# A retention and feed-forward kernel: the first weight tiles and item loads in another order, later loads of q and k, and one subtraction moved in the A stages

## The chip, the cores and the metric

The kernel runs on one core of a Trainium2 chip. The metric is the device time of one execution in microseconds. Three runs of the kernel before took 859.01, 855.62 and 859.25 us, median 859.01 us. TensorE (PE, and PEld for its weight loads) multiplies; VectorE (DVE), ScalarE (ACT) and GpSimd (POOL) work on tiles; SyncE (SP) issues nearly all DMAs, ACT a few.

## The reference

```python
scores = np.matmul(q, k.transpose(0, 1, 3, 2)) / np.sqrt(D)      # q, k, v: 8 batches, 8 heads, 576 positions, 64
gamma = 1.0 - 2.0 ** (-5.0 - np.arange(H))
Dmat = np.where(rel >= 0, gamma[:, None, None] ** rel, 0.0)      # rel = position of q - position of k
x = np.matmul(scores * Dmat, v)                                  # then 4608 tokens x 512
h = x @ w_in                                                     # w_in: 512 x 2048
out = (h - np.tanh(h)) @ w_out                                   # w_out: 2048 x 512
```

All inputs and the output are float32.

## The kernel before

The 576 positions are cut into nine chunks of 64. An *item* is one batch in one chunk; eight items make a block of 512 tokens. Retention is computed chunk by chunk: scores inside the chunk, masked by the decay, times v, plus q times a state that the chunks before have left. Float32 products on TensorE are made of two words each: a high word (`xh`, `gh`, the first of `win`) and a low word (the rest, by a subtraction on DVE), three products a term.

**The start.** `load_first` (line 560) loads item j of chunk 0 into `a`; the masks' table `decay` and item 1 go through ACT's queue, everything else through SP's. TensorE first runs matmuls on a zero tile `warm` (`busy`, line 551). Then for each j the loop at line 596 runs the scores of item j + 2 together with the product of item j (`run`, line 300), multiplies scores by the decay (`after_score`, DVE, line 308) and copies the product to `xh` on ACT and its remainder to `xl` on DVE (`after_out`, lines 326 to 329). Meanwhile `load_w` (line 96) loads the tiles of `w_in`, each 128 x 512 of 8 bytes. A tile is made into words in steps: `guard` (two activations on ACT, lines 106 and 111), three bit operations on DVE (lines 137, 145 and 147, in `unit`), a rounded copy on ACT (line 153), and the subtraction for the low word on DVE (line 166, `finish`). `step` does the next piece of that work wherever it is called, so its place in the program is its place in each engine's order. Tile 1 has a function of its own, `second` (lines 124 to 129). Then `mm1` (line 447) multiplies a block by a tile of `w_in`, 12 matmuls of 128 x 512; the program for chunks 0 and 1 runs 32 of these with steps of the tiles to come between them. `behind` makes a DMA wait for a named instruction, and `pace` holds the names.

**The later stages.** Chunks 3 to 8 are handled in pairs: a stage A (`stage_a`) computes the hidden layer of two chunks together from seven products (`product`, line 917) of half blocks, and a stage B (`stage_b`) computes the output of the second chunk while it prepares the next two by attention steps (`attend`). In stage A, pair j leaves two of its four hidden tiles (`c12`, `c22`) in memory and splits the other two into words at once; the fourth of pair 0 (`c21`) is split in a function `rest` that waits in `pending` for pair 1. `u2` and `u4` are sums kept in the tile `work`. In stage B, each step f runs the 12 matmuls of `mm2` (line 503); an even step begins with an attention step. `load_turn` (line 801) loads q and k (in an even step) or v (odd) for an attention step three turns ahead, and is held by a matmul of the step's `mm2`; `fetch` (line 472) loads a hidden tile `s` for four steps ahead, behind it on SP's queue. `scale_q` (line 255) and `split` (lines 932, 933) are the first users of these.

In all of this each engine executes its instructions in the order of the program.

Of the kernel before, what the change touches and what calls it, by code (L numbers as in the profile page):

```python
# [9 lines left out]
F32 = mybir.dt.float32  # L10
F32R = mybir.dt.float32r
I32 = mybir.dt.int32
BF16 = mybir.dt.bfloat16
AF = mybir.ActivationFunctionType
ALU = mybir.AluOpType
# [59 lines left out]
def retention_ffn(ctx: ExitStack, tc: tile.TileContext, ins, out, spill, wvar):  # L75
# [36 lines left out]

    halves = (slice(0, DM // 2), slice(DM // 2, DM))

    def second(low):

        t, f = stream[1]
        hw, lw, z = wraw[t, f][:, :, 1], wraw[t, f][:, :, 0], masks.pop((t, f))
        del wraw[t, f]

        w = const.tile([P, 2, 2, DM // 2], F32R, tag="wi14", name="wi1")
        win[f] = w
        upto("guard", 3)
        nc.vector.scalar_tensor_tensor(z, hw, 3, z, op0=ALU.logical_shift_left, op1=ALU.bitwise_and)
        low()
        nc.vector.scalar_tensor_tensor(z, lw, 29, z, op0=ALU.logical_shift_right, op1=ALU.bitwise_or)
        nc.vector.scalar_tensor_tensor(z, hw, -0x40000000, z, op0=ALU.bitwise_and, op1=ALU.bitwise_or)
        for n, at in enumerate(halves):
            nc.scalar.copy(w[:, n, 0], z[:, at].bitcast(F32))  # L129
        last.append(("i", w, z))  # L130

    def unit(k):

# [29 lines left out]
    def finish():  # L163
        while last:
            hi, lo, full = words_of(*last.pop())
            nc.vector.tensor_tensor(lo, full, hi.bitcast(F32), op=ALU.subtract)
# [7 lines left out]
    def upto(what, n):  # L174
        while at_[what] < min(n, 2 * NF):
            {"load": load_w, "guard": guard}[what](*stream[at_[what]])
            at_[what] += 1
# [117 lines left out]
    def run(same, other):  # L295

        while same or other:
            for ms in (same, other):
                for out_, w, x, start, stop in ms[:2]:
                    nc.tensor.matmul(out_, w, x, start=start, stop=stop)  # L300
                del ms[:2]
# [249 lines left out]
    def busy(n, cols):  # L551
        for _ in range(n):
            nc.tensor.matmul(wps[:, :cols], warm[:, :P], warm[:, :cols], start=True, stop=True)

    busy(WARM, 140)
    busy(8, BLK // 2)
    decay = const.tile([P, 4, C], F32, tag="wo7", name="decay")
    krows = [const.tile([P, 4, 4, D], F32, tag=f"wo{4 + t}", name=f"krows{t}") for t in range(2)]

    def load_first(j, queue=nc.sync):  # L560
        loaded[j] = const.tile([P, 3, 4, C], F32, tag=f"wo{NF - 1 - j}", name=f"a{j}")
        queue.dma_start(loaded[j], first_d[j])

    load_first(0)
    nc.scalar.dma_start(decay, decay_d)
    load_first(1, nc.scalar)
    load_first(2)
    upto("load", 1)
    load_first(3)
    load_first(4)  # L570
    load_first(5)
    nc.scalar.activation(warm[:, :1], warm[:, :1], AF.Tanh)

    firsts, lows = {}, []

    def score_first(j):
        firsts[j] = psp.tile([P, 8, C], F32, tag=("o0", "o1", "h")[j % 3], bufs=(1, 1, 2)[j % 3], name=f"s_first{j}")
        firsts[j] = firsts[j][:, :4]  # L580
        return m_score(j, firsts[j])

    def paced(load):

        pace.append(tc.nc.cur_bb.bb.instructions[-1].name)
        load()

    def load_paced(j):
        load_first(j)
        behind(tc, pace[-1])  # L590

    run(score_first(0), [])
    after_score(0, firsts[0].unsqueeze(1), 1)
    run(score_first(1), [])
    after_score(1, firsts[1].unsqueeze(1), 1)
    for j in range(B):
        o = psp.tile([P, 8, C], F32, tag=("o2", "o3", "own")[j % 3], bufs=1, name=f"own_first{j}")[:, :4]
        run(score_first(j + 2) if j < B - 2 else [], m_out(j, o))
        if j == 0:
            paced(lambda: load_paced(6))  # L600
        if j == 1:
            paced(lambda: load_paced(7))
        if j < B - 2:
            after_score(j + 2, firsts[j + 2].unsqueeze(1), 1)
            if 0 < j < 5:
                paced(lambda: upto("load", j + 1))
        if j == 4:
            nc.sync.dma_start(vtab, vtab_d)
            nc.sync.dma_start(krows[0], krows_d[0])
            load_pair(B)  # L610
            nc.sync.dma_start(mask, mask_d)
            upto("load", 7)
            load_pair(B + 2)
        if j == 3:
            busy(6, BLK)
        if 0 < j < 4:
            step()
        low = after_out(j, o.unsqueeze(1), 1, False)
        if j == 0:
            upto("guard", 1)  # L620
        if j == 3:
            step()
        if j == 5:
            finish()
            guard(*stream[1], both=False)
        if j < 7:
            low()
        else:
            guard_end(masks[stream[1]])
            at_["guard"] = 2  # L630
    units(1)
    second(low)
    at_["convert"] = 2

    def scale_k(t):
# [319 lines left out]
    def stage_a(na):  # L955

        nb, pending = na + 1, []
        u2, u4 = work[:, 0], work[:, 1]
        for j in range(NPAIR):
            x, y = [psp.tile([P, BLK], F32, tag=t, bufs=1, name=f"p{t}{na}_{j}") for t in ("new" if j else "o0", "own")]  # L960
            z, v = [psp.tile([P, BLK], F32, tag="h", bufs=2, name=f"p{t}{na}_{j}") for t in "zv"]
            f1, f2 = 2 * j, 2 * j + 1
            c22, c12, c21 = [pool.tile([P, BLK], F32, tag="g", bufs=3, name=f"c{t}_{na}_{j}") for t in (22, 12, 21)]

            def tanh(c):
                th = pool.tile([P, BLK], F32, tag="cv", bufs=4, name=f"th{na}_{j}")
                nc.scalar.activation(th, c, AF.Tanh)  # L967
                return th

            def away(c, f):  # L970
                nc.gpsimd.tensor_tensor(c, c, tanh(c), op=ALU.subtract)  # L971
                nc.sync.dma_start(spill[nb, f], c)

            product(0, x)
            product(1, y)
            nc.scalar.copy(u2, x)
            nc.vector.tensor_tensor(u2, y, u2, op=ALU.add)  # L977
            product(2, z)
            nc.vector.tensor_tensor(u4, z, u2, op=ALU.add)
            while pending:  # L980
                pending.pop()()
            product(3, v)
            nc.vector.tensor_tensor(c22, v, u4, op=ALU.add)  # L983
            y = psp.tile([P, BLK], F32, tag="own", bufs=1, name=f"py{na}_{j}")
            product(4, y)
            away(c22, f2)
            nc.vector.tensor_tensor(c12, y, u4, op=ALU.add)
            product(5, x, False)
            away(c12, f1)
            g11 = tanh(x)  # L990
            nc.vector.tensor_tensor(g11, x, g11, op=ALU.subtract)
            product(6, v, False)
            split(na, f1, g11, False)
            nc.vector.tensor_tensor(c21, v, u2, op=ALU.add)

            def rest(f=f2, c=c21, tanh=tanh):
                nc.vector.tensor_tensor(c, c, tanh(c), op=ALU.subtract)
                split(na, f, c, True)

            if j == 0:  # L1000
                pending.append(rest)
            else:
                mm2_pair(na, j - 1)
                rest()
        for f in range(3):
            fetch(nb, f)
        mm2_pair(na, NPAIR - 1)
        for f in range(2):
            split(nb, f, fetched.pop((nb, f)), False)
# [5 lines left out]
    def stage_b(n, m0):  # L1015

        fetch(n, 3)
        for f in range(NF):
            def ahead():
                if f + 2 < NF:  # L1020
                    split(n, f + 2, fetched.pop((n, f + 2)), f % 3 == 0)

            if n == 2 and f == 1:
                load_tables(FIRST)
            m, odd = m0 + f // 2, f % 2 == 1
            if n < NC - 1 and not odd:
                attend(m, ahead)
            else:
                ahead()
            if n == NC - 1:  # L1030
                fetch_on(n, f + 4)
            if n == 2 and f == NF - 1:
                load_slot(2)
            if (n, f) != (NC - 1, NF - 2):
                names = mm2(n, f)
            if n < NC - 1:
                load_turn(m + 3 - odd, int(odd), names[6 if odd else 2])
                fetch_on(n, f + 4)
            if odd and tables:
                load_tables(tables.pop())  # L1040
                set_tables()
            if n == 2 and f == 2:
                set_tables()
            if n == 2 and 9 < f < 15:
                load_slot(*((0, f - 10) if f < 14 else (1,)))
# [87 lines left out]
```

## Time and profile before

| | |
|---|---|
| median of three runs | 859.01 us (855.62 to 859.25) |
| the profiled execution's own time | 856.53 us |
| its span | 854.8 us |
| TensorE busy | 843.2 us (99%), 7701 matmuls |
| DVE, ACT, POOL busy | 57%, 43%, 9% |
| granted TensorE clock | full throughout |
| DMA | 174.67 MB, mean 204 GB/s |

The span runs from the first to the last instruction; the execution's time has 1.7 us around it. A row of the timeline gives start and duration in microseconds, the engine, the source line, the operation, the tile written and those read, the shape, how many instructions were merged (x12), and in brackets how long the engine had been idle and what ended that. A row of the waits gives who waited for whom, the total in microseconds, how many times, and the longest. A row of the DMA issues ends with the median time from issue to landing. `SPq` marks instructions that issue DMAs.

### The profile page before, as it was taken

To read this page: it belongs to the slowest core of one execution; us is meant where nothing else is said; L and a number is where in the kernel's file an instruction comes from. 1 tells how busy PE (TensorE), PEld (TensorE's weight loads), DVE (VectorE), ACT (ScalarE), POOL (GpSimd) and SP (SyncE) were. 2 spreads that over 40 slices of the span, in tenths; PEclk is the share of its full clock that TensorE was granted. 3 is DMA by queue.
4 is the path that set the end of the run, shared out by engine and by line. 5 is a ranking of instruction groups with operands and counts; after the bars stand their busy time and mean duration, and the time that the engine had idled before them with its cause. 6 is when DMAs were issued, how large, how long until landed. Compare 5 with 4: busy or idle time off the path is not lost.

```text
span 854.8 us, 18569 instructions
## 1 busy us (share of the span) xinstructions
PE 843.2 (99%) x7701; PEld 695.2 (81%) x7702; DVE 484.6 (57%) x817; ACT 364.4 (43%) x723; POOL 74.3 (9%) x63
## 2 busy tenths in 40 slices
PE   7999999999999999999999999999999999999998
PEld 6888888887888787888888788888888888888886
DVE  5989877868567665434346754434456554343321
ACT  4887774444234553323244443322345433232321
POOL 0001001110000001212110002211100012121100
PEclk9999999999999999999999999999999999999999
DMA  9976968776777579435376665534666255352432
GB/s 340 364 244 205 365 222 277 239 235 202 234 259 289 188 252 326 163 130 190 123 235 213 205 184 199 182 132 173 208 207 215 90 184 185 128 192 74 138 109 74
DMA packets 62404, 174.67 MB, mean 204 GB/s; under 512 B 7536, under 2 KB 8944, under 8 KB 57072
## 3 DMA queue, kind: packets, MB, share of 16 engines
q1 hardware_dynamic: 61792, 172.57, 59.5%
q8 instruction: 60, 0.98, 0.5%
q10 hardware_dynamic: 528, 0.92, 0.3%
q14 instruction: 24, 0.20, 0.1%
HBM read 124.70 MB, written 48.76 MB: 203 GB/s over the span
## 4 chain that ended last, share of the span: by engine, by line
PE 87%; issue 4%; DMA 4%; DVE 2%; ACT 1%; SPq 0%; POOL 0%; DVEq 0%; POOLq 0%; ACTq 0%
PE o L503 25%; PE o L948 15%; PE h L447 15%; PE pv L917 7%; PE pnew L917 6%; PE py L917 4%; PE pz L917 4%; PE pown L917 4%; PE s L300 3%; DMA s<-spill_dram 2%; PE new L300 2%; PE own L300 2%; DMA a<-in_first_dram 1%; PE po L917 1%; DMA rwi<-in_w_in_dram 1%
## 5 line engine op out<-in xcount | busy, mean ns | idle before, releaser
L503 PE MATMUL o<-wo,gh 128*128 128x512 f32 x608 | 156.8, 395 | 0.3 <-ACT gh L484 0.3
L503 PEld LDWEIGHTS o<-wo,gh 128*128 128x128 f32 x608 | 111.8, 188 | 26.8 <-ACT gh L484 2.2
L971 POOL TENSOR_TENSOR c<-c,th 128x512 f32<-128x512 f32 x48 | 62.0, 1297 | 516.6 <-ACT th L967 515.5
L967 ACT ACTIVATE th<-c 128x512 f32<-128x512 f32 x72 | 45.5, 632 | 140.9 <-DVE c L983 89.7
L447 PE MATMUL h<-xh,wi 128*128 128x512 f32 x384 | 97.7, 392 | 0.8 <-ACT xh L326 0.5
L447 PEld LDWEIGHTS h<-xh,wi 128*128 128x128 f32 x384 | 71.3, 188 | 16.9 <-ACT wi L129 0.8
L503 PE MATMUL o<-wo,gl 128*128 128x512 f32 x304 | 84.2, 389 | 0.0
L948 PE MATMUL o<-wo,gs 128*128 128x512 f32 x288 | 70.7, 389 | 0.0
L503 PEld LDWEIGHTS o<-wo,gl 128*128 128x128 f32 x304 | 57.1, 188 | 11.9
L948 PEld LDWEIGHTS o<-wo,gs 128*128 128x128 f32 x288 | 54.1, 188 | 11.2
L917 PE MATMUL pv<-xhv,ws 128*128 128x512 f32 x192 | 59.2, 390 | 0.6 <-DVE c L983 0.6
L503 PE MATMUL o<-wo,gs 128*128 128x512 f32 x240 | 59.2, 394 | 0.0
L300 PE MATMUL own<-qk,state 64*64 64x64 f32 x928 | 57.1, 221 | 0.0
L300 PE MATMUL own<-qk,vr 64*64 64x64 f32 x928 | 56.1, 218 | 0.7 <-issue 0.7
L977 DVE TENSOR_TENSOR work<-pown,work 128x512 f32<-128x512 f32 x24 | 16.6, 692 | 67.8 <-PE pown L917 67.1
L503 PEld LDWEIGHTS o<-wo,gs 128*128 128x128 f32 x240 | 44.4, 188 | 9.5
L917 PE MATMUL pnew<-xhv,ws 128*128 128x512 f32 x168 | 51.7, 389 | 0.0
L447 PE MATMUL h<-xl,wi 128*128 128x512 f32 x192 | 51.6, 389 | 0.0
L948 PE MATMUL o<-wo,gh 128*128 128x512 f32 x192 | 48.9, 389 | 0.0
L300 PEld LDWEIGHTS own<-qk,vr 64*64 64x64 f32 x928 | 46.6, 135 | 0.1
L300 PEld LDWEIGHTS own<-qk,state 64*64 64x64 f32 x928 | 46.2, 134 | 0.4 <-issue 0.4
L933 DVE TENSOR_TENSOR gl<-s,gh 128x512 fp32r<-128x512 f32 x44 | 30.0, 688 | 23.9 <-ACT gh L932 12.1
(152 smaller groups left out, 1516.4 us busy)
## 6 DMA issues: line engine op xcount, KB each, us to landing
ws<-wvar_dram SPq DMA_DIRECT2D x41, 1024.0 KB, 4.7
s<-spill_dram SPq DMA_DIRECT2D x94, 256.0 KB, 3.8
qk<-in_qkv_dram SPq DMA_DIRECT2D x29, 512.0 KB, 4.2
vr<-in_qkv_dram SPq DMA_DIRECT2D x29, 512.0 KB, 3.9
spill_dram<-c SPq DMA_DIRECT2D x48, 256.0 KB, 2.3
spill_dram<-g SPq DMA_DIRECT2D x36, 256.0 KB, 3.5
rwi<-in_w_in_dram SPq DMA_DIRECT2D x16, 512.0 KB, 5.6
rwo<-in_w_out_dram SPq DMA_DIRECT2D x16, 512.0 KB, 5.5
```

Of the source, the lines that this page charges most:

```text
L300: nc.tensor.matmul(out_, w, x, start=start, stop=stop)
L447: nc.tensor.matmul(hp, win[f][:, cc // 2, a, cc % 2 * P : (cc % 2 + 1) * P], x[:, cc, :], start=(k == 0), stop=(k == 3 * NCC - 1))
L503: nc.tensor.matmul(ops[n][t], g[:, t * P : (t + 1) * P], wout[f_][:, a, :], start=(f_ == first and k == 0), stop=(f_ == final and k == 2),)
L917: nc.tensor.matmul(into, w[:, a, k], x[:, k], start=start and i == 0, stop=i == len(terms) - 1, skip_group_check=not start,)
L933: nc.vector.tensor_tensor(gl, g, gh.bitcast(F32), op=ALU.subtract)
L948: nc.tensor.matmul(ops[n][t], g[:, t * P : (t + 1) * P], wout[f][:, a, :], start=(j == 0 and f == fs[0] and k == 0), stop=last_,)
L967: nc.scalar.activation(th, c, AF.Tanh)
L971: nc.gpsimd.tensor_tensor(c, c, tanh(c), op=ALU.subtract)
L977: nc.vector.tensor_tensor(u2, y, u2, op=ALU.add)
```

## The change

It has four parts. (1) At the start weight tile 0 is issued first, items 0 to 4 behind it on SP; items 5 to 7 and weight tiles 1 to 4 wait each for the last matmul of a step. The conversion of tile 0 is spread over the first steps, ahead of the masks; a warm matmul of full width follows each of the first six steps, in place of a block behind step 3. (2) `second` does tile 1 in two halves, guards included, behind the last item, and finishes its low word itself. (3) In stage A pair 1's `c22` comes ahead of what pair 0 left in `pending`, and `u2` alternates between two places. (4) In even steps of stage B the load of q and k is released by the twelfth matmul of the step, and no longer by the third.

```diff
-    def second(low):
+    def second():
         t, f = stream[1]
-        hw, lw, z = wraw[t, f][:, :, 1], wraw[t, f][:, :, 0], masks.pop((t, f))
-        del wraw[t, f]
+        raw, z = wraw.pop((t, f)), masks.setdefault((t, f), pool.tile([P, DM], I32, tag="cv", bufs=4, name=f"m{t}{f}"))
+        del masks[t, f]
...
-        upto("guard", 3)
-        nc.vector.scalar_tensor_tensor(z, hw, 3, z, op0=ALU.logical_shift_left, op1=ALU.bitwise_and)
-        low()
-        nc.vector.scalar_tensor_tensor(z, lw, 29, z, op0=ALU.logical_shift_right, op1=ALU.bitwise_or)
-        nc.vector.scalar_tensor_tensor(z, hw, -0x40000000, z, op0=ALU.bitwise_and, op1=ALU.bitwise_or)
+        for at in halves:
+            nc.scalar.activation(z[:, at], raw[:, at, 1].bitcast(F32), AF.Tanh, scale=STEP)
+            nc.scalar.activation(z[:, at].bitcast(F32), z[:, at], AF.Abs, scale=HI_BITS)
         for n, at in enumerate(halves):
-            nc.scalar.copy(w[:, n, 0], z[:, at].bitcast(F32))
+            m, hw, lw = z[:, at], raw[:, at, 1], raw[:, at, 0]
+            nc.vector.scalar_tensor_tensor(m, hw, 3, m, op0=ALU.logical_shift_left, op1=ALU.bitwise_and)
+            nc.vector.scalar_tensor_tensor(m, lw, 29, m, op0=ALU.logical_shift_right, op1=ALU.bitwise_or)
+            nc.vector.scalar_tensor_tensor(m, hw, -0x40000000, m, op0=ALU.bitwise_and, op1=ALU.bitwise_or)
+            nc.scalar.copy(w[:, n, 0], m.bitcast(F32))
+            if n == 0:
+                guard(*stream[2], both=False)
+        guard_end(masks[stream[2]])
+        at_["guard"] = 3
         last.append(("i", w, z))
+        finish()
...
     busy(WARM, 140)
-    busy(8, BLK // 2)
+    busy(8, BLK)
...
-    load_first(0)
+    upto("load", 1)
     nc.scalar.dma_start(decay, decay_d)
-    load_first(1, nc.scalar)
-    load_first(2)
-    upto("load", 1)
-    load_first(3)
-    load_first(4)
-    load_first(5)
-    nc.scalar.activation(warm[:, :1], warm[:, :1], AF.Tanh)
+    for j in range(5):
+        load_first(j)
+    upto("guard", 1)
...
     run(score_first(0), [])
+    step()
     after_score(0, firsts[0].unsqueeze(1), 1)
     run(score_first(1), [])
+    paced(lambda: load_paced(5))
+    step()
     after_score(1, firsts[1].unsqueeze(1), 1)
     for j in range(B):
...
         run(score_first(j + 2) if j < B - 2 else [], m_out(j, o))
+        if j < 2:
+            paced(lambda: load_paced(6 + j))
+        elif j < B - 2:
+            paced(lambda: upto("load", j))
+        if j < B - 2:
+            busy(1, BLK)
         if j == 0:
-            paced(lambda: load_paced(6))
-        if j == 1:
-            paced(lambda: load_paced(7))
+            step()
         if j < B - 2:
             after_score(j + 2, firsts[j + 2].unsqueeze(1), 1)
-            if 0 < j < 5:
-                paced(lambda: upto("load", j + 1))
-        if j == 4:
+        after_out(j, o.unsqueeze(1), 1)
+        if j == 0:
+            step()
+        if j == 1:
+            finish()
+        if j == 5:
...
-        if j == 3:
-            busy(6, BLK)
-        if 0 < j < 4:
-            step()
-        low = after_out(j, o.unsqueeze(1), 1, False)
...
-    units(1)
-    second(low)
+    second()
...
-        u2, u4 = work[:, 0], work[:, 1]
+        u4 = work[:, 1]
         for j in range(NPAIR):
+            u2 = work[:, 3 * (j % 2)]
...
+            product(3, v)
+            nc.vector.tensor_tensor(c22, v, u4, op=ALU.add)
             while pending:
                 pending.pop()()
-            product(3, v)
-            nc.vector.tensor_tensor(c22, v, u4, op=ALU.add)
...
-                load_turn(m + 3 - odd, int(odd), names[6 if odd else 2])
+                load_turn(m + 3 - odd, int(odd), names[6 if odd else 11])
```

More of the change, by code (lines that the diff above doesn't have):

```diff
@@ L562, in load_first @@
         queue.dma_start(loaded[j], first_d[j])
-    load_first(0)
+    upto("load", 1)
     nc.scalar.dma_start(decay, decay_d)
-    load_first(1, nc.scalar)
-    load_first(2)
-    upto("load", 1)
-    load_first(3)
-    load_first(4)
-    load_first(5)
-    nc.scalar.activation(warm[:, :1], warm[:, :1], AF.Tanh)
-    firsts, lows = {}, []
+    for j in range(5):
+        load_first(j)
+    upto("guard", 1)
+    firsts = {}
     def score_first(j):
@@ L613, in retention_ffn @@
             load_pair(B + 2)
-        if j == 3:
-            busy(6, BLK)
-        if 0 < j < 4:
-            step()
-        low = after_out(j, o.unsqueeze(1), 1, False)
[L619 to L630, printed above, removed]
-    units(1)
-    second(low)
+    assert not going and not last
+    second()
     at_["convert"] = 2
```

## The prediction

> **What bounds the kernel now.** I read the page first, then who TensorE waited for, then the timeline of the three places that the change touches.
>
> ```profile
> PE 843.2 (99%) x7701; PEld 695.2 (81%) x7702; DVE 484.6 (57%) x817; ACT 364.4 (43%) x723; POOL 74.3 (9%) x63
> ```
>
> ```profile
> PE s_first L300 <- DMA a<-in_first_dram: 2.9, 5, 1.3
> ...
> PE pv L917 <- DVE c L983: 0.6, 1, 0.6
> ```
>
> TensorE is busy 843.2 of 854.8 us. Its 11.6 us of idle time lie almost all in the first 20 us, with one wait of 0.6 us in the first A stage. No edit removes a matmul of the result, so the change can only win idle time, and there is little of it. The start decides:
>
> ```profile
> 8.81 0.27 PE L300 MATMUL s_first<-a 64*64 64x64 f32 x2 [0.72 <-DMA a<-in_first_dram]
> ...
> 9.79 0.27 PE L300 MATMUL s_first<-a 64*64 64x64 f32 x2 [0.28 <-DMA a<-in_first_dram]
> ...
> 14.05 0.27 PE L300 MATMUL s_first<-a 64*64 64x64 f32 x2 [0.41 <-DMA a<-in_first_dram]
> ...
> 16.47 2.11 PE L447 MATMUL h<-xh,wi 128*128 128x512 f32 x8 [0.51 <-ACT xh L326]
> ...
> 19.82 0.73 PE L447 MATMUL h<-xh,wi 128*128 128x512 f32 x2 [0.33 <-ACT wi L129]
> ...
> 22.83 0.76 PEld L447 LDWEIGHTS h<-xh,wi 128*128 128x128 f32 x4 [0.42 <-ACT wi L153]
> ```
>
> Until 14.05 the scores wait for items `a` to land; item 7 is the last. Then follow item 7's mask, its own product, its copy to `xh`, and at 16.47 the first `mm1` of 12 matmuls. The second could have come 12 x 0.234 + 0.1 = 2.9 us later, at 19.35, and comes at 19.82, when half of tile 1's high word is there; the third waits at 22.83 for tile 2's.
>
> **The change, part by part.** *Order of the loads.* Ahead of item 3 stand the same bytes before and after (decay, items 0 to 2, weight tile 0: 1.8 MB), only in another order. Item 3 therefore lands when it did (score 3 at 8.81), and so does item 4 (9.79): 0.98 us an item. Items 5, 6 and 7 are issued by the last matmul of the score of item 1, of step 0 and of step 1. Item 7 was already issued by step 1's last matmul:
>
> ```profile
> 9.58 0.33 SPq L562 DMA_DIRECT2D a<-in_first_dram  x1
> 10.04 0.35 SPq L96 DMA_DIRECT2D rwi<-in_w_in_dram  x1
> ```
>
> ```profile
> q1 hardware_dynamic: 244, 0.70, 101.9%
> q8 instruction: 1, 0.02, 3.4%
> ```
>
> The second fence is the DMA view of 10.5 to 12.5 us. The load of item 7 takes 14.05 - 9.58 = 4.5 us, while 384 KB at the page's rate are done in one; in this stretch one instruction load sits on one engine for 3.4% of 16 engines x 2 us = 1.1 us, and that engine's share of item 7 and of tile 1 comes late. TensorE reaches the same instruction count at about the same time after the change (three warm matmuls earlier), so I keep 14.0 for item 7 and the old landing of tile 1, about 15.2 (5.13 us after its issue, by the chain row in the next fence), though its issue moves half a microsecond back to step 2's end. [...]
>
> The conversion of tile 0 now runs as soon as tile 0 is there, ahead of mask 0 on DVE: one operation of 0.68 us before each of the first three masks. Four items follow tile 0 up to item 3, so tile 0 lands near 8.8 - 4 x 0.98 = 4.9; two guard operations of 0.68 us (the row at 15.20 below) and one of DVE bring mask 0 to 7.0. It is wanted when item 2 lands, at 7.8; masks 1 and 2 follow in the same way, each one operation behind its item and ahead of the next but one. Cost nothing, covered by the loads; uncovered it would be 0.6 us. The longer first warm burst costs 8 x 0.11 us and ends near 5.8, when item 0 lands behind tile 0. The warm matmuls at full width that stood in one block between steps 3 and 4 are now one per step (0.22 us each) and lie in waits for items. All in all the first `mm1` stays at about 16.4; I book -0.05.
>
> *Tile 1 in halves.* These rows are ACT and DVE, with one row of the chain of waits ahead:
>
> ```profile
> 10.04 5.13 DMA rwi<-in_w_in_dram
> ```
>
> ```profile
> 15.20 0.68 ACT L106 ACTIVATE mi<-rwi 128x512 int32<-128x512 f32 x1
> 15.78 0.64 ACT L326 CAST xh<-own_first 128x256 fp32r<-128x256 f32 x2
> ...
> 16.98 0.69 DVE L124 SCALAR_TENSOR_TENSOR mi<-rwi,mi 128x512 int32<-128x512 int32 x1 [0.38 <-ACT mi L111]
> 17.59 0.42 DVE L329 TENSOR_TENSOR xl<-own_first,xh 128x256 fp32r<-128x256 f32 x1
> ...
> 18.64 0.69 DVE L127 SCALAR_TENSOR_TENSOR mi<-rwi,mi 128x512 int32<-128x512 int32 x1
> 19.25 0.68 DVE L137 SCALAR_TENSOR_TENSOR mi<-rwi,mi 128x512 int32<-128x512 int32 x1
> 19.36 0.71 ACT L129 CAST wi<-mi 128x256 fp32r<-128x256 f32 x2 [1.18 <-DVE mi L127]
> ...
> 20.11 0.69 DVE L166 TENSOR_TENSOR wi<-mi,wi 128x512 fp32r<-128x512 f32 x1 [0.17 <-ACT wi L129]
> 20.71 0.69 DVE L145 SCALAR_TENSOR_TENSOR mi<-rwi,mi 128x512 int32<-128x512 int32 x1
> 21.44 0.69 DVE L147 SCALAR_TENSOR_TENSOR mi<-rwi,mi 128x512 int32<-128x512 int32 x1
> ...
> 22.16 0.62 ACT L153 CAST wi<-mi 128x512 fp32r<-128x512 f32 x1 [0.37 <-DVE mi L147]
> ```
>
> Before, ACT guarded tile 1 from 15.20, between the last copies to `xh`; after, it starts behind the last copy, at 16.3. No row shows the half operations; the nearest are those on 128x256, 0.42 us on DVE (17.59) and 0.64 us for two back to back on ACT (15.78), so under 0.4 for one. Guard of a half: 0.4 + 0.35, so the first half's bits can start at 17.1; three dependent half operations at 0.42 + 0.03 end at 18.45, its copy at 18.85. The second `mm1` then starts at 19.35 without its wait: -0.47. The second half: DVE to 19.7, and its copy, with one guard operation of tile 2 ahead of it on ACT, to 20.1; it is wanted after four matmuls, at 20.25. The low word is subtracted at 20.15, ending 20.85, wanted at 21.2. All three fit, the second by 0.15 us.
>
> What this does to tile 2: before, its first operation (L137, 19.25) ran on DVE while DVE waited for the copies, ahead of the subtraction at 20.11. After, the subtraction is the last thing in the function for tile 1, and tile 2's first operation comes behind it and behind the second half of its guard (ACT, 20.0 to 20.65). Subtraction 20.15, then 20.75, 21.48, 22.2 for the three operations (the spacings 0.6 and 0.72 are those from 20.11 to 20.71 to 21.44), and the copy from 22.9: TensorE has the third `mm1` at about 23.55 where it had 22.83. **The -0.5 of the second `mm1` is given back, and 0.7 us lost.** DVE queues behind it everything of tile 3 on, but from there both orders are equal and TensorE never waited again, so the start costs +0.7. Lower bound -0.6 (item 7 lands 1.3 us sooner without the slow engine), upper bound +1.3 (tile 0 late by the 0.6 us above).
>
> *Second pair's c22.*
>
> ```profile
> 334.99 0.68 DVE L994 TENSOR_TENSOR c<-pv,work 128x512 f32<-128x512 f32 x1
> 336.38 0.69 DVE L977 TENSOR_TENSOR work<-pown,work 128x512 f32<-128x512 f32 x1 [0.71 <-ACT work L976]
> ...
> 337.78 0.68 DVE L997 TENSOR_TENSOR c<-c,th 128x512 f32<-128x512 f32 x1
> 339.15 0.69 DVE L933 TENSOR_TENSOR gs<-c,gs 128x512 fp32r<-128x512 f32 x1 [0.69 <-ACT gs L932]
> 339.95 0.69 DVE L983 TENSOR_TENSOR c<-pv,work 128x512 f32<-128x512 f32 x1
> ```
>
> ```profile
> 339.53 0.61 PE L917 MATMUL pnew<-xhv,ws 128*128 128x512 f32 x2
> 340.69 0.73 PE L917 MATMUL pv<-xhv,ws 128*128 128x512 f32 x2 [0.55 <-DVE c L983]
> ```
>
> `c22` (L983) stood behind the first pair's rest (L997, L933); now it comes ahead, at 337.8 at the latest, and `u2` alternates between two places, so its copy no longer waits for L994. The seventh product then starts at 339.99 instead of 340.69: **-0.7** (two matmuls of 0.23 after 339.53). The rest moves behind by one operation of 0.6 us, to 340.3 at worst; its product in `mm2` comes after seven groups of matmuls more, 342 at the soonest. Bounds -0.7 and 0.
>
> *q and k later.* In 21 steps the load of q, k and the fetch `s` queued behind it on SP move back by nine matmuls, 9 x 0.234 = 2.1 us.
>
> ```profile
> 286.20 0.33 SPq L801 DMA_DIRECT2D qk<-in_qkv_dram  x1
> 286.94 0.33 SPq L472 DMA_DIRECT2D s<-spill_dram  x1
> ...
> 294.32 0.68 DVE L255 TENSOR_TENSOR qk<-qk,work 128x512 f32<-128x512 f32 x1
> ```
>
> ```profile
> 294.78 0.64 ACT L932 CAST gh<-s 128x512 fp32r<-128x512 f32 x1
> ```
>
> ```profile
> s<-spill_dram SPq DMA_DIRECT2D x94, 256.0 KB, 3.8
> qk<-in_qkv_dram SPq DMA_DIRECT2D x29, 512.0 KB, 4.2
> ```
>
> `qk` lands at 290.4 and is used at 294.32; `s` lands at 290.7 and is used at 294.78. Of 4 us in hand 2 stay. Cost 0. What it may move are the two gaps of TensorE inside the attention steps that no engine explains:
>
> ```profile
> 293.11 0.27 PE L300 MATMUL new<-vr 64*64 64x64 f32 x2 [0.49 <-issue]
> ```
>
> ```profile
> 483.94 0.21 PE L300 MATMUL own<-qk,vr 64*64 64x64 f32 x1 [0.68 <-issue]
> ```
>
> Together 1.2 us; bounds -1.2 if both go, +1.2 if two more come.
>
> **Sum:** +0.7 - 0.7 + 0 = 0.0 against the profiled execution (856.53 us, of which 854.8 span and 1.7 around it), bounds -2.5 and +2.5. That execution lies 2.5 below the median of the three runs, which spread over 3.6 us by themselves (855.62 to 859.25). The mean of all four is 857.6, and I forecast that.
>
> **The rivals.** *The start gains:* item 7 lands at 12.7, near the rate of the items before it. Then all of the start moves 1.3 sooner, +0.7 becomes -0.6, and the time is 856.3. For it: item 7's own bytes could end then. Against: the instruction load falls due at the same matmul count. *The gaps go:* moving q and k away from the attention step frees both issue gaps, 856.4. Against: v keeps its place and loads there still. *Tile 0 delays the items* (the table of Tanh loaded only when tile 0 lands, say): +0.6, 858.2. *Slower:* q, k and `s` now enter the queues right ahead of the next attention step, which spends instructions fastest, and TensorE's own instruction load is late behind them. At 0.49 to 0.68 us a gap, it needs seven gaps more to reach 4.3 us; in 15 of 24 steps it would be 9 us, 866. For it: the two gaps lie in just these steps. Against: 22 of 24 steps have none, though v and `s` load there now. [...] *The c22 edit does nothing:* 858.3.
>
> **How the numbers follow.** Forecast 0.50, start gains 0.17, gaps go 0.13, tile 0 delays 0.11, slower 0.05, c22 nothing 0.04. The bounds of 2.5 about 857.6 give 855.1 to 860.1; with the spread of the runs, which a median of few halves at best, 854.0 to 860.6. About 0.5% (4.3 us) is what a measurement of this kernel tells from no change. All cases but one stay inside it; the gains together with a low set of runs might pass it: faster 0.09, same 0.86, slower 0.05.
>
> **What would show it.** First `mm1` at 16.4 (start gains: 15.2); second 2.9 us later without a wait; third waiting for tile 2's copy near 23.5; L983 of the second pair ahead of L997 and no wait of `pv` in the first A stage; no wait for `qk` or `s`. I am wrong about tile 2 if the third `mm1` starts before 22.8, and about the whole if TensorE shows new issue gaps in most attention steps.

## The result, and the profile after

The changed kernel takes 863.7 us (median of six runs, 861.09 to 865.58), the kernel before 856.25 us (six runs, 855.06 to 859.25). The ratio is 1.0088, with a 95% interval of 1.0065 to 1.0110: **7.5 us slower.** The forecast was no change, 857.6 us, with 854.0 to 860.6 as its range.

The profiled execution took 861.88 us, with a span of 860.1 us against 854.8. First the page's line of busy times, then who TensorE waited for:

```profile
PE 844.6 (98%) x7699; PEld 695.9 (81%) x7702; DVE 486.2 (57%) x820; ACT 365.0 (42%) x724; POOL 74.6 (9%) x63
```

```profile
PE own L307 <- issue: 2.7, 2, 1.5
PE s_first L307 <- DMA a<-in_first_dram: 2.3, 3, 1.4
PE new L307 <- issue: 1.6, 1, 1.6
PE h L454 <- ACT wi L160: 1.3, 1, 1.3
PE wps L560 <- DVE warm L554: 1.2, 1, 1.2
PE o L510 <- issue: 0.7, 1, 0.7
```

TensorE is busy 1.4 us longer than before (844.6 against 843.2), and 4 us more idle time stand between its instructions. Nearly all of that is marked *issue*: it waited for nothing that this view shows. Where the time is lost is read off the same place of the program in both traces. These are the first `mm1`, the first B stage's first `mm2` and the first A stage's first product, of the kernel before and then of the changed one:

```profile
16.47 2.11 PE L447 MATMUL h<-xh,wi 128*128 128x512 f32 x8 [0.51 <-ACT xh L326]
...
262.13 0.50 PE L503 MATMUL o<-wo,gh 128*128 128x512 f32 x1
...
322.27 0.61 PE L917 MATMUL po<-xhv,ws 128*128 128x512 f32 x2
```

```profile
17.30 2.12 PE L454 MATMUL h<-xh,wi 128*128 128x512 f32 x8 [0.47 <-ACT xh L333]
...
24.59 0.74 PE L454 MATMUL h<-xh,wi 128*128 128x512 f32 x2 [1.30 <-ACT wi L160]
...
263.01 0.50 PE L510 MATMUL o<-wo,gh 128*128 128x512 f32 x1
...
325.74 0.39 PE L911 MATMUL po<-xhv,ws 128*128 128x512 f32 x1
```

The lead of the kernel before is 0.8 us at the first `mm1`, 0.9 us when the first B stage begins, and 3.5 us when it ends. So the first B stage alone costs 2.6 us in these two executions. The issue gaps of the changed kernel lie in the three B stages:

```profile
287.50 0.74 PE L510 MATMUL o<-wo,gh 128*128 128x512 f32 x2 [0.67 <-issue]
...
296.05 0.27 PE L307 MATMUL new<-vr 64*64 64x64 f32 x2 [1.59 <-issue]
...
487.60 0.21 PE L307 MATMUL own<-qk,vr 64*64 64x64 f32 x1 [1.23 <-issue]
...
647.75 0.33 PE L307 MATMUL own<-qk,vr 64*64 64x64 f32 x2 [1.50 <-issue]
```

The kernel before had two of them, 0.49 and 0.68 us, at 293.11 and 483.94: the same two attention steps as the second and third here. The changed kernel has four, up to 1.6 us long.

### The profile page after: what moved, and what is told of

It is laid out like the page before. It is cut to its first block, busy times and chain, and to the rows that moved or that the text cites. A ratio compares the mean times of both kernels' runs of the same rounds, so it can differ in the third digit from the quotient of the medians.

```text
span 860.1 us, 18566 instructions
## 1 busy us (share of the span) xinstructions
PE 844.6 (98%) x7699; PEld 695.9 (81%) x7702; DVE 486.2 (57%) x820; ACT 365.0 (42%) x724; POOL 74.6 (9%) x63
## 4 chain that ended last, share of the span: by engine, by line
PE 90%; issue 5%; DMA 2%; DVE 2%; ACT 1%; POOL 0%; SPq 0%; POOLq 0%; DVEq 0%; ACTq 0%
PE o L510 26%; PE o L942 15%; PE h L454 15%; PE pv L911 7%; PE pnew L911 6%; PE py L911 4%; PE pz L911 3%; PE pown L911 3%; PE s L307 3%; PE new L307 2%; PE own L307 2%; DMA s<-spill_dram 2%; PE wps L560 1%; PE po L911 1%; DMA a<-in_first_dram 1%
```

## The experiments

Each kernel was timed in turn with the kernel before on the same chip; ratios are against that.

**1. The pacing undone in the changed kernel, and 2. the pacing alone on the kernel before.**

```diff
 # e1_pace_back, on the changed kernel
-                load_turn(m + 3 - odd, int(odd), names[6 if odd else 11])
+                load_turn(m + 3 - odd, int(odd), names[6 if odd else 2])
 # e2_pace_alone, on the kernel before: the same edit the other way
```

> The changed kernel with one edit undone: q and k of an even step are released by the third matmul again. Theory (late instruction loads): the new gaps of TensorE inside the B stages, 0.8, 1.8, 0.4, 1.4 and 1.7 us in the profile after, come from the loads moved in front of the attention steps; undone, TensorE has again two gaps there of about 0.7 and 0.9 us, and the time falls by some 4.5 us to about 859, which leaves the start's loss of 1 to 3 us against the kernel before. Rival (the new order of the start displaces the rest, or the gaps come by chance): the time stays within 1 us of 863.7 and gaps of over 1 us remain.

> The kernel before with that one edit alone: q and k released by the twelfth matmul. Theory: gaps of 0.4 to 1.8 us appear in the attention steps, four to six of them, and the time rises by about 4.5 us, to 860 to 861. Rival: no new gaps, time within 1 us of 856.3.

Undone, the changed kernel takes 857.74 us, ratio 1.0021 (1.0008 to 1.0035). Alone on the kernel before, the pacing takes 862.95 us against 856.73, ratio 1.0086 (1.0059 to 1.0113). This one index makes most of the loss, 6.0 us by the difference of the medians of the changed kernel with and without it (863.70 and 857.74, measured at different times) and 6.2 us alone, 1.5 us more than the gaps of one profile had let expect. The gaps come and go with it. Here are TensorE's waits marked issue in the B stages, of the first kernel and then of the second:

```profile
PE new L307 <- issue: 0.8, 1, 0.8
...
PE own L307 <- issue: 0.4, 1, 0.4
```

```profile
PE own L300 <- issue: 3.1, 2, 2.1
...
PE new L300 <- issue: 1.6, 1, 1.6
...
PE o L503 <- issue: 0.3, 1, 0.3
```

The longest gap of the second kernel, 2.05 us, ends at 487.91, and 1.1 us behind it the granted clock halves for 3.4 us. With v sooner (experiment 7) the same follows a gap of 2.31 us that ends at 647.02. These are the rows of both (length, busy time of PE, PEld, DVE, ACT and POOL, then the clock, the share of the DMA engines and GB/s):

```profile
489.00:492.40 3.40, 3.40 (x10) 2.62 (x9) 3.28 (x8) 3.18 (x11) 0.00 (x0) 0.50 0.02 7
```

```profile
648.60:652.00 3.40, 3.40 (x10) 2.62 (x9) 1.63 (x4) 2.11 (x6) 0.00 (x0) 0.50 0.67 216
```

At half the clock 3.4 us of matmuls lose 1.7 us, an estimate from the 0.50 of these rows. The span of the pacing alone is 6.7 us above the kernel before's (861.5 against 854.8): 3.8 are gaps, 1.7 the clock, and 1.2 a later first `mm1` (17.63 against 16.47).

**3. The start alone.**

```diff
 # e3_start_alone: the changed kernel without parts (3) and (4)
-            u2 = work[:, 3 * (j % 2)]
...
-                load_turn(m + 3 - odd, int(odd), names[6 if odd else 11])
+                load_turn(m + 3 - odd, int(odd), names[6 if odd else 2])
```

> The kernel before with the whole change of the start (order of loads, warm matmuls, tile 0 in the first steps, tile 1 in halves) and nothing else. Theory (tile 2 is late): the third group of twelve matmuls starts 1 to 2 us later than before, and the time rises by 1 to 2 us. A second theory for the start (the clock): with the block of warm matmuls spread out, TensorE's clock falls back in some executions; then some of the runs show a granted clock of 0.993 to 0.998 and 2 to 4 us more than the others, as four of the six runs of the changed kernel do. Rival: the start changes nothing, within 0.5 us.

858.05 us against 856.73, ratio 1.0019 (1.0006 to 1.0031): the start costs 1.3 us. The third group of twelve matmuls starts 24.92 - 17.64 = 7.28 us behind the first; before it was 22.83 - 16.47 = 6.36. The second theory, the clock, falls: the kernel before shows a granted clock of 0.995 to 0.998 in 7 of its 29 runs and the new start one of 0.997 or 0.998 in 2 of 12, so a lower clock in some runs is no mark of the new start.

```profile
17.64 2.11 PE L454 MATMUL h<-xh,wi 128*128 128x512 f32 x8 [0.47 <-ACT xh L333]
...
24.92 0.97 PE L454 MATMUL h<-xh,wi 128*128 128x512 f32 x3 [1.32 <-ACT wi L160]
```

**4. The edit of the A stage alone.**

```diff
 # e4_c22_alone, on the kernel before
-        u2, u4 = work[:, 0], work[:, 1]
+        u4 = work[:, 1]
         for j in range(NPAIR):
+            u2 = work[:, 3 * (j % 2)]
...
+            product(3, v)
+            nc.vector.tensor_tensor(c22, v, u4, op=ALU.add)
             while pending:
                 pending.pop()()
-            product(3, v)
-            nc.vector.tensor_tensor(c22, v, u4, op=ALU.add)
```

> The kernel before with the edit of the A stage alone. Theory: the wait of 0.7 us ahead of the seventh product in the first A stage goes, time -0.4 to -0.7 us. Rival: it is hidden or returns later, within 0.2 us.

856.71 us against 856.73, ratio 0.9998 (0.9983 to 1.0012). The wait of `pv` for `c22` (L983) is absent from its trace, but it is absent from four traces without the edit too (experiments 3, 7, 10 and 11), and 0.2 to 0.6 us long in the others. The interval of 2.5 us is too wide to tell 0.7 us from nothing, so the gain in time is not shown. The three parts alone, 6.2, 1.3 and 0.0 us, add up to the 7.5 us of the whole change.

**5. Traffic alone, ahead of the attention step, and 10. the same traffic inside it.**

```diff
 # e5_traffic_alone, on the kernel before, behind fetch_on(n, f + 4)
+                if not odd and m + 3 < len(turns):          # e10_traffic_later: if odd and ...
+                    c_, b_ = divmod(turns[m + 3], B)
+                    nc.sync.dma_start(
+                        scratch[m], qkv_d[c_ - 1, ORDER[c_].index(b_) // 2, 0].rearrange("p n w i s -> p (n w i s)"),
+                    )
+                    behind(tc, names[11])
```

> The kernel before, with q, k and every other load where they were; in each even step of the B stages one more transfer of 512 KB is added, from memory to memory, which nobody reads, released by the step's twelfth matmul. It tells two readings of the pacing's loss apart. Theory (crowded queues delay TensorE's instruction loads): the gaps marked issue appear though all data come as before, at least three of over 1 us, and the time rises by 4 us or more. Rival (q, k or s come too late for their first users): no new gaps, time within 1.5 us of 856.7.

> The same added transfers of 512 KB as in the run with the added traffic, as many and as large, but released by the twelfth matmul of the odd step, that is into the attention step itself and not ahead of it. Theory (what counts is the backlog while the instruction packet is asked for, in the odd step): nearly no loss, within 1.5 us of 856.5. Rival (any added traffic costs this much): again 863.

With 21 transfers that nobody reads, released where the changed kernel releases q and k, the time is 863.27 us against 856.53, ratio 1.0078 (1.0055 to 1.0102). No load was moved. TensorE's waits in that kernel:

```profile
PE py L917 <- DMA ws<-wvar_dram: 1.9, 1, 1.9
PE own L300 <- issue: 1.7, 2, 1.0
...
PE new L300 <- issue: 1.0, 1, 1.0
```

So traffic at that place is enough to lengthen the gaps though all data come as before. The expectation was too simple in its detail: the issue gaps are three, 0.71 to 1.04 us, and sum to 2.7 us, 1.5 more than in the kernel before. The rest of this kernel's loss is of another kind: a wait of 1.9 us for the tile `ws`, one of 0.6 us for q scaled, and 3.4 us at half the clock behind the first of these, none of which the profile after has at that length. So the size of its loss, near that of the pacing, is in part a coincidence. The same 21 transfers released one step later, at the odd step's last matmul, cost 858.82 us against 856.89, ratio 1.0023 (1.0007 to 1.0038), and the issue gaps are no longer than those of the kernel before:

```profile
PE s L300 <- DVE qk L255: 1.3, 2, 0.7
...
PE new L300 <- issue: 0.5, 1, 0.5
...
PE own L300 <- issue: 0.4, 1, 0.4
```

Its loss of 1.9 us is 0.4 more than was allowed for, and of another kind: in two attention steps the scores wait for q scaled on DVE (1.3 us). Between these two runs it is the place of the bytes that counts, far more than their number.

**6. Halfway.**

```diff
 # e6_pace_middle, on the kernel before
-                load_turn(m + 3 - odd, int(odd), names[6 if odd else 2])
+                load_turn(m + 3 - odd, int(odd), names[6])
```

> The kernel before with q and k released by the seventh matmul of an even step, between the third of the kernel before and the twelfth of the changed one. Theory (the bytes must be through before the next attention step): part of q, k and s now falls into it, and the time lies between, 857.5 to 861. Rival (a threshold of lateness alone): as before, within 1 us of 856.7.

856.95 us against 856.53, ratio 1.0004 (0.9987 to 1.0021): no loss that can be measured, which is what the rival expected and less than the theory did. The profile has one longer gap (1.3 us, against 0.5 before) at the usual place; the other two in the B stages sum to 0.6 us, and two of 0.3 us stand among the `mm1`, at 43 and 64 us, which the profile before doesn't have. Four matmuls' delay is nearly free; nine are not, and this run by itself doesn't say why. (Its longer gap stands behind an instruction packet that began on time but took 1.84 us, where the kernel before's took 1.23; such packets are the matter of the list below.)

**7. v sooner, and 11. v later.**

```diff
 # e7_v_sooner, on the kernel before
-                load_turn(m + 3 - odd, int(odd), names[6 if odd else 2])
+                load_turn(m + 3 - odd, int(odd), released if odd else names[2])
+                released = names[11]
 # e11_v_later
+                load_turn(m + 3 - odd, int(odd), names[11 if odd else 2])
```

> The kernel before with v's load of an odd step released by the last matmul of the even step ahead, seven matmuls (1.6 us) sooner; q and k stay with the third. Theory (crowded queues): v's bytes are through when the attention step begins, the gaps of 0.7 and 0.9 us of the kernel before go, and the time falls by 1 to 1.6 us, to about 855.4. Rival (the gaps have another cause): they stay, time within 0.5 us of 856.7.

> The kernel before with v of the odd step released by its twelfth matmul in place of its seventh, 1.2 us later. With v sooner the time rose by 5 us. Theory (backlog in the odd step): v's bytes leave the odd step for the attention step, the gaps get no longer than before and may shrink, time 855.5 to 857, as far as v comes in time. Rival (moving v in either direction hurts, since v or s come too late): 859 and more.

The first expectation was wrong in its sign: 861.45 us against 856.53, ratio 1.0051 (1.0035 to 1.0067), with the longest gaps of all:

```profile
PE own L300 <- issue: 4.1, 2, 2.3
PE new L300 <- issue: 1.9, 1, 1.9
...
PE o L503 <- issue: 0.4, 1, 0.4
```

v sooner brings v's bytes into the odd step, behind q, k and `s`, as q and k later do. The first form of the theory, that the bytes must be through when the attention step begins, falls with it. v later takes them out of the odd step: 856.27 us against 856.89, ratio 0.9987 (0.9973 to 1.0000), which is no loss and no gain that can be told from none; its gaps are 0.76 and 0.41 us.

The packets of the instruction queue say what the gaps wait for. This list is taken from the packet and instruction records of the traces. The fifth column is the time from the packet's end until TensorE goes on; the last says how many of TensorE's instructions lie between the one it starts when the packet begins and the one it stops at:

```
run                packet of 16 KB, us   TensorE resumes   gap    from packet's end   ahead
before             290.51 to 291.74      293.11            0.68   1.37                210
before             481.50 to 482.44      483.94            0.87   1.51                211
after              285.13 to 286.07      287.50            0.83   1.43                113
after              293.68 to 294.71      296.05            1.77   1.34                77
after              485.18 to 486.16      487.60            1.42   1.44                131
after              645.00 to 646.24      647.75            1.69   1.50                136
pacing alone       484.74 to 486.42      487.91            2.24   1.50                123
traffic ahead      291.22 to 292.18      293.40            1.23   1.22                125
v sooner           644.71 to 645.60      647.02            2.50   1.42                0
v later            294.31 to 295.26      296.60            0.95   1.34                180
```

The gap here is the start-to-start time less its usual size. In all six kernels TensorE goes on 1.2 to 1.5 us after such a packet has ended, at the same four places of the program, and the gap is by and large longer where the packet begins later in the program: 210 instructions ahead in the kernel before, 77 to 136 in the changed one (its first, 113 ahead with a gap of 0.83 us, is the exception). The places themselves speak for missing instructions. Counted over all of TensorE's records, its sequencer's among them, the stops come at 6,080, 6,336, 10,176 and 12,736 instructions, to within two, and each of these is 192 above a multiple of 256. So it is for 47 of the 53 waits marked issue in the fourteen traces; the other six are of 0.16 us, in the first 12 us. The DMA view shows the packet against the traffic. First the kernel before, 290.4 to 291.8 us; then the changed kernel, 290.4 to 293.6 and 293.6 to 294.8 us:

```profile
q1 hardware_dynamic: 58, 0.24, 56.6%
q8 instruction: 1, 0.02, 5.5%
```

```profile
q1 hardware_dynamic: 271, 0.79, 78.3%
q14 instruction: 1, 0.01, 0.9%
```

```profile
q1 hardware_dynamic: 115, 0.37, 100.5%
q8 instruction: 1, 0.02, 5.4%
```

In the kernel before the packet finds the data queue just over half busy. In the changed one, where q and k, `s`, v and `s` again are issued within 2 us, TensorE is 210 instructions ahead of the stop at 292.40; the packet begins at 293.68, 1.3 us later, and beside a full data queue. The issues themselves:

```profile
290.10 0.33 SPq L795 DMA_DIRECT2D qk<-in_qkv_dram  x1
290.85 0.33 SPq L479 DMA_DIRECT2D s<-spill_dram  x1
291.69 0.33 SPq L795 DMA_DIRECT2D vr<-in_qkv_dram  x1
292.11 0.38 SPq L479 DMA_DIRECT2D s<-spill_dram  x1
```

The count fits q8 holding TensorE's instructions: by the page of the changed kernel it has 60 packets of 16 KB, and TensorE's rows number 7,699 + 7,702 = 15,401, which is 257 a packet; the first two of the stops lie 256 apart.

**8. Tile 2's first operation ahead again.**

```diff
 # e8_tile2_ahead, on the start alone (3)
+        at_["guard"] = 2
         for at in halves:
             nc.scalar.activation(z[:, at], raw[:, at, 1].bitcast(F32), AF.Tanh, scale=STEP)
             nc.scalar.activation(z[:, at].bitcast(F32), z[:, at], AF.Abs, scale=HI_BITS)
+        upto("guard", 3)
...
-            if n == 0:
-                guard(*stream[2], both=False)
-        guard_end(masks[stream[2]])
-        at_["guard"] = 3
         last.append(("i", w, z))
-        finish()
```

> The changed start alone, with one order mended: tile 2's guard stands whole ahead of the copies of tile 1, and tile 2's first operation on DVE comes ahead of tile 1's subtraction again. Theory (tile 2 is late by that order): the third group of twelve matmuls starts about 6.6 us behind the first and no longer 7.3, and the time falls by about 0.6 us against the changed start alone, 858.05, to 857.4. Rival: 7.3 us as before.

The third group now starts 24.04 - 17.28 = 6.76 us behind the first, against 7.28; its wait for tile 2's copy is 0.67 us and no longer 1.32. The time is 857.45 us against 856.53, ratio 1.0009 (0.9996 to 1.0021). The order explains about half of the wait; what is left of the start's loss can't be told from none here.

```profile
17.28 2.12 PE L451 MATMUL h<-xh,wi 128*128 128x512 f32 x8 [0.47 <-ACT xh L330]
...
24.04 1.21 PE L451 MATMUL h<-xh,wi 128*128 128x512 f32 x4 [0.67 <-ACT wi L157]
```

**9. q and k sooner, and 12. the edits without a loss together.**

```diff
 # e9_qk_sooner, on the kernel before
-                load_turn(m + 3 - odd, int(odd), names[6 if odd else 2])
+                load_turn(m + 3 - odd, int(odd), names[6] if odd else None)
 # e12_best, on the kernel with the A stage's edit (4)
+                load_turn(m + 3 - odd, int(odd), names[11] if odd else None)
```

> The kernel before with q and k of an even step held by nothing but their buffer, so that they are issued when the attention step ends, some 0.5 us sooner. In the runs so far each gap marked issue in the B stages ends 1.2 to 1.5 us after a 16 KB packet of the instruction queue, at the same four places of the program, and that packet starts when the loads queued ahead of it are through. Theory (the backlog in the odd step delays that packet): with q, k and s through sooner the packet near 290 us starts up to 0.5 us sooner, the gaps of 0.7 and 0.9 us shrink by as much, and the time falls by 0.5 to 1 us against 856.5. Rival (chance): gaps as before.

> The three edits that did not lose, together, on the kernel before: the second pair's c22 sooner, q and k held by their buffer alone, v released by the twelfth matmul of the odd step. If their gains of 0 to 0.6 us add up, 855.3 to 856, about 1 us under the kernel before. Rival (each was scatter): within 0.5 us of 856.7.

q and k sooner: 856.41 us against 856.89, ratio 0.9991 (0.9978 to 1.0004), and the two gaps stand in its profile as they stood before, 0.7 and 0.5 us idle; the expected shrinking did not come, so sending q and k sooner does not relieve the packets of the kernel before. The expectation has the packet start when the loads queued ahead of it are through. By the semaphore records the four packets of the changed kernel in the list begin within 0.15 us of the landing of q and k, but 0.6 to 1.0 us ahead of that of the `s` behind them; the two of the kernel before begin 0.8 and 1.2 us behind the landing of q and k. All three together: 856.06 us against 856.27, ratio 0.9995 (0.9981 to 1.0009). No version beats the kernel before by more than the measurement can tell.

## Why the prediction was wrong

**The step that failed** is "q and k later", with its "Cost 0", and with it the bound of 1.2 us. The step looked at the data: q and k and `s` had 4 us in hand, 2.1 were spent, 2 would stay. For the data that nearly holds: in the profile after, one score waits 0.3 us for q scaled on DVE, and no other matmul for anything that the moved loads bring. The step left out that TensorE's own instructions, by the counts above, come as DMA packets too, 60 of 16 KB, and that the moved loads fill the data queue in the odd step, just where such a packet stands: it was busy 78% and 100% in the two stretches of the changed kernel under the list, 57% in that of the kernel before. The term measured +6.2 us alone and +6.0 us undone. Its bounds took the gaps to be 1.2 us in all, to go or to double; measured, they sum to 5.0 us in the profile after. The two issue gaps of the kernel before were quoted beside the step, and read as something that might go or come in the same size. They were the mark of the mechanism: places where the instruction packet was already late by 0.5 to 0.7 us, with nothing in hand.

**The slower rival** named this mechanism and had it at 0.05. It was underrated in two ways. Its price was taken from the gaps of before, 0.49 to 0.68 us, so that seven more gaps were wanted; each of those late by the queues got longer instead, to 1.2 to 1.6 us idle in the changed kernel and 2.3 in another. And it spoke against itself that 22 of 24 attention steps had no gap: the stops of the list stand at fixed counts, each 192 above a multiple of 256, and only the few steps where such a count falls among the small matmuls, or just behind them, lost. What it lost was not many gaps more but the same ones, longer, and two new ones. The idle time marked issue at the four rows after sums to 5.0 us, that of before to 1.2, a difference of 3.8 us in this one execution. The runs lose more, and the granted clock goes with it: the two runs of the changed kernel at 1.000 took 861.09 and 861.88 us, the four at 0.993 to 0.998 took 862.64 to 865.58. In the kernels of experiments 2 and 7 the clock halves behind the longest gap (0.50 for 3.4 us); in the changed kernel no profile has caught that.

**The start.** The sum was +0.7 us; alone it measured 1.3 us, at the upper bound; its interval, 0.5 to 2.7 us, holds the 0.7. The reason held for the larger part: tile 2 is late by its order behind tile 1's subtraction. Its third group was to start 23.55 - 16.4 = 7.15 us behind the first, and started 7.28 behind it where the start stood alone; with the order mended, 6.76, against 6.36 in the kernel before. Two smaller readings were off. The first warm burst was to end near 5.8; in the profile after it ran until 6.97:

```profile
1.19 5.78 PE L560 MATMUL wps<-warm 128*128 128x140 bf16 x32 [1.19 <-DVE warm L554]
```

In that execution the burst's matmuls of full width start 0.43 us apart until 6.1 us and 0.21 apart behind it, so most of them ran at half the later speed; what stood behind the burst moved back with it. The late share of item 7, with which the prediction kept its old landing, is there in both traces: its load raises its semaphore in 16 steps, of which the fifteenth came at 12.62 us and the last at 13.91 in the kernel before, ahead of the score at 14.05, and at 13.48 and 14.60 in the changed one, ahead of the score at 14.73. The instruction packet of that stretch ran from 10.90 to 11.97 us and from 10.73 to 11.69. The first `mm1` came at 17.30 and not at 16.4. But 16.47 was an early execution: over the ten traces with the old start it came at 16.47 to 18.50, over the four with the new one at 17.28 to 18.16, so 0.9 us of the first `mm1` proves nothing about the order of the loads. In four of the ten a gap marked issue of 1.2 to 2.1 us lies ahead of it (experiments 2, 9, 11 and 12).

**c22.** In the four traces with the edit `pv` never waits for `c22`, as the step said; but of the ten without it four don't wait either, so the 0.7 us was the price of one execution. That the edit saves 0.7 us of time is neither shown nor refuted; 0.7 us is under 0.1%.

**Item 7 and the gaps as rivals.** "The start gains" and "the gaps go" did not happen; v stayed where it was, and the gaps grew.

**Open.** When exactly TensorE asks for a packet, and what delays the two packets of the kernel before, is not shown: the profile shows the packet, not the request. Nor is it shown whether the packet waits in a queue or for the memory behind it. Moving the instruction count itself, with a few added matmuls, would have been the run for it. That a long gap brings the clock down is only seen together with it: a gap of 2.1 us in the start of experiment 12 had no such fall.

## What to carry to other kernels

Where TensorE runs through many small matmuls, ask what its instruction stream needs from the DMA engines, and read a wait marked issue as a place without slack: a load that is moved must be checked against it, and not only against the first user of its data. Look for the place of the bytes, not their sum: the same 21 transfers cost 6.7 us in one step, stalls for data and a slower clock among them, and 1.9 us in the next. And when a price is taken from two gaps, ask whether the cause makes more of them or makes them longer.

## What the runs showed of the hardware that was not expected

At the ten stops of the list TensorE went on 1.2 to 1.5 us after the end of an instruction packet of 16 KB, in the six kernels alike. Releasing 512 KB per pair of steps, and the `s` queued behind it, some 2 us later cost 0.86% (experiment 2), while the mean data rate hardly moved (204 GB/s by the page of before, 203 by that of the pacing alone).

The granted clock fell in the start of an execution as well. In the profile of experiment 4, which has the old start, the stretches of 10 to 15 and 15 to 20 us (columns as in experiment 2):

```profile
10.00:15.00 5.00, 3.26 (x101) 2.21 (x102) 4.68 (x11) 1.96 (x5) 0.00 (x0) 1.00 0.96 297
15.00:20.00 5.00, 3.93 (x68) 3.50 (x69) 2.82 (x7) 3.24 (x7) 0.00 (x0) 0.66 1.00 384
```

The clock is at 0.66 of its speed in the mean between 15 and 20 us, where the first `mm1` begins. Runs with a lower mean clock were longer, in the kernel before too: of its first 29 the seven at 0.995 to 0.998 have a median of 859.04 us, the other 22 one of 856.3, and the four longest, 859.04 to 859.94 us against a median of 856.73, are among the seven. They make up part of its spread of 5 us.
